# Moving one unit's attention product among the state products, and one state update to an earlier slot, in a fused linear-attention and bilinear FFN kernel

## The chip, the cores and the metric

The kernel runs on one core of one Trainium2 chip. The metric is the device time of one execution in microseconds (us); lower is better. Engines are named as in the profile: PE is TensorE, DVE is VectorE, ACT is ScalarE, POOL is GpSimd, SP is SyncE, which issues nearly all DMAs.

## The reference

Attention over blocks of 64 positions with a decaying state, for 4 batches, 8 heads, 768 positions and head size 64; then a bilinear FFN over the 3072 rows of width 512 with inner width 1536:

```python
for b in range(nb):
    intra = np.einsum('bhic,bhjc->bhij', qb, kb) * Dmask[None]
    intra = np.einsum('bhij,bhjd->bhid', intra, vb)
    inter = np.einsum('bhid,bhde->bhie', qb * lam_pow[None], kv_state)
    out[:, :, sl] = intra + inter
    kv_state = lam_block[None, :, None, None] * kv_state + np.einsum('bhsd,bhse->bhde', kb_dec, vb)
...
return (a * b @ w_out).astype(np.float32)   # a = x @ w_a, b = x @ w_b
```

## The kernel before

The kernel works in blocks of 128 positions, six to a batch: 24 units, numbered 0 to 23. q and k are scaled by powers of lam beforehand, so that the decay drops out of the products: the scores need only a lower-triangular mask, and the state of a unit is the plain sum of k-transposed times v over the units of its batch so far. For each unit there are: the scores kq (line 309, or 561 for the first four units) in two PSUM banks, one for the even and one for the odd heads; the mask m, a DVE product that brings them to SBUF (line 321); the intra product, v times masked scores, eight small column-tiled matmuls (line 346); the inter product, four matmuls with the state of the unit before (line 336); the evacuation of both into xT, the FFN's input (line 353 on ACT, 355 on DVE); and the kv update, four full matmuls (line 360) or eight column-tiled ones (`kv_beside`, line 381), that add to the running sum in one PSUM bank, kvd, followed by `kv_copy`, which takes that sum to SBUF as the unit's state (line 390 on ACT in two halves, line 392 on DVE).

The FFN goes over groups of units (4, 1, 2, 4, 4, 4, 4, 1). For each of 12 slices f of the inner width it makes a (line 428, evacuated by ACT at line 435) and b (line 428, multiplied with a by DVE into ab at line 440), then the output product op (line 449, evacuated by ACT at line 444 and stored). While the FFN of one group runs, the attention work of later units is put between its matmuls by hand: `PLAN` gives for each group pairs of a slot (f, or 12 and on for the halves of the output product) and a piece of work. "P" scales and converts a unit's q, k and v, "T" transposes q and k, "S" makes scores and masks, "V" is the kv update with its copy, "O", "O2" and "Q" are the inter and intra products and evacuations of one or two units, "Q" with the scores and masks of the next two. Each engine executes its instructions in the order in which the program issues them.

PSUM has eight banks: seven are handed out in turn, or at a number given by hand (`at=`), and the eighth holds kvd. A tile that gets a bank waits until the former tile there has been read.

The start phase (lines 505 to 623) does units 0 to 3 before any FFN work, with idle matmuls (`warm`, line 193) on PE between its steps. Lines 599 to 611, the place of the change: the second half of the scores; then the kv products of units 0, 1 and 2, each as a sum of its own over the units up to it (in bank 3, bank 1 and kvd), first the lower two head pairs for all three, then the upper two, with the copies (ACT, ACT, DVE); then the intra products, the inter products and the four evacuations. The fourth mask reads bank 1. The first FFN product needs all four evacuations. In group 2 (units 5 and 6 in the FFN), slot 7 has the kv update of unit 7, slot 12 the "Q" of units 7, 8, 9 and 10, slot 13 the kv update of unit 9 and slot 14 the "O2" of units 9 and 10; the update of unit 8 is made inside `pieces_O` after the intra products:

```python
        if len(us) == 2 and us[0] >= n0 + 3:
            kv_beside(us[1])
        for u, kq in zip(nxt, kqs):
            masks(u, kq)
        if len(us) == 2 and us[0] >= n0 + 3 and us[1] % NB < NB - 1:
            kv_copy(us[1], kv["ps"])
```

Here n0 is 4 and NB is 6.

Of the kernel before, what the change touches and what calls it, by code (L numbers as in the profile page):

```python
# [22 lines left out]
def _bc(ap, dims):  # L23
# [20 lines left out]
    1: [(0, "V", 4), (2, "T", 5), (3, "PK", 6), (6, "PV", 6), (6, "S", 5), (7, "T", 6),  # L44
        (10, "S", 6), (12, "O2", (5, 6)), (13, "P", 7)],
    2: [(0, "V", 6), (1, "T", 7), (1, "P", 8), (4, "T", 8), (5, "P", 9), (6, "S", 7),
        (6, "S", 8), (7, "V", 7), (8, "P", 10), (10, "T", 9), (11, "T", 10),
        (12, "Q", (7, 8, 9, 10)), (12, "P", 11), (13, "V", 9), (14, "P", 12),
        (14, "O2", (9, 10))],
    3: [(3, "S", 11), (3, "S", 12)],  # L50
# [12 lines left out]
def kernel(  # L63
# [12 lines left out]
    B, H, S, D = q.shape  # L76
    BLK = 128
    NB = S // BLK
# [27 lines left out]
    def ps_bank(name, shape, dt, hold=False, ffn=False, at=None):  # L106
        i = bank["next"] if at is None else at
        while i in bank["held"] or (ffn and i == bank["ffn"]):
            i = (i + 1) % 7
        if ffn:  # L110
            bank["ffn"] = i
        bank["next"] = (i + 1) % 7
        if hold:
            bank["held"].add(i)
        return ps_pool.tile(shape, dt, name=name, tag=f"ps{i}")
# [52 lines left out]
    n0 = GROUPS[0]  # L168
# [24 lines left out]
    def warm(n, cols=128):  # L193
        for _ in range(n):
            nc.tensor.matmul(idle_ps[:, :cols], lhsT=idle_sb[:, :128], rhs=idle_sb[:, :cols],  # L195
                             start=True, stop=True, skip_group_check=True)
# [103 lines left out]
    def score_banks():  # L300
        return [ps_bank(f"kq{i}", [128, HP, 128], F32) for i in range(2)]

    def scores(u, kq=None):
        d = U[u]
        kq = kq or score_banks()
        for hp in range(HP):
            for i in range(2):
                p = slice(64 * i, 64 * i + 64)
                nc.tensor.matmul(kq[i][:, hp, :], lhsT=d["kT"][p, hp, :], rhs=d["qT"][p, hp, :],  # L309
                                 start=True, stop=True, skip_group_check=True)  # L310
        return kq

    def masks(u, kq):
        ms = mask(kq)
        U[u]["m"] = lambda i, hp: ms[i][:, hp, :]
# [9 lines left out]
    def o_bank(u):  # L325
        first = "o" not in U[u]
        if first:
            U[u]["o"] = ps_bank("o_ps", [128, HP, 128], F32)
        return first

    def inter(u):
        d = U[u]
        if u % NB > 0:
            first = o_bank(u)
            for hp in range(HP):
                nc.tensor.matmul(d["o"][:, hp, :], lhsT=st_bufs[(u - 1) % 4][:, hp, :, :],  # L336
                                 rhs=d["qT"][:, hp, :], start=(first and hp == 0), stop=True,
                                 skip_group_check=True)

    def intra(u, first=False):  # L340
        d = U[u]
        first = o_bank(u) or first
        for hp in range(HP):
            for i in range(2):
                p = slice(64 * i, 64 * i + 64)
                nc.tensor.matmul(d["o"][p, hp, :], lhsT=d["vb"][:, 2 * hp + i, :],  # L346
                                 rhs=d["m"](i, hp), start=(first and hp == 0),
                                 stop=True, skip_group_check=True)

    def evac_o(u, xT, col, eng="act"):  # L350
        o_ps = U[u].pop("o")
        if eng == "act":
            nc.scalar.copy(xT[:, :, col:col + BLK], o_ps)  # L353
        else:
            nc.vector.tensor_copy(xT[:, :, col:col + BLK], o_ps)

    def kv_mms(ps, w, hps, first):
        d = U[w]
        for hp in hps:
            nc.tensor.matmul(ps[:, hp, :, :], lhsT=d["kn"][:, 2 * hp:2 * hp + 2, :],  # L360
                             rhs=d["vb"][:, 2 * hp:2 * hp + 2, :], start=(first and hp == 0),
                             stop=True, skip_group_check=True)
# [12 lines left out]
    def kv_beside(u):  # L375
        if u % NB == 0 or u % NB == NB - 1:
            kv_update(u)
        for hp in range(HP if 0 < u % NB < NB - 1 else 0):
            for i in range(2):
                p = slice(64 * i, 64 * i + 64)  # L380
                nc.tensor.matmul(kv["ps"][p, hp, i, :], lhsT=U[u]["kn"][:, 2 * hp + i, :],
                                 rhs=U[u]["vb"][:, 2 * hp + i, :],
                                 start=False, stop=True, skip_group_check=True)

    def kv_copy(u, ps, eng="dve"):
        st = st_bufs[u % 4]
        if eng == "act":
            for i in range(2):
                p = slice(64 * i, 64 * i + 64)
                nc.scalar.copy(st[p, :, i, :], ps[p, :, i, :])  # L390
        else:
            nc.vector.tensor_mul(st[:].rearrange("p hp i d -> p hp (i d)"),  # L392
                                 ps[:].rearrange("p hp i d -> p hp (i d)"), bdiag_bc)
# [11 lines left out]
    def pieces_O(us, nxt=()):  # L405
        kqs = [score_banks() for u in nxt]
        for u in us:
            inter(u)
        for u, kq in zip(nxt, kqs):
            scores(u, kq)  # L410
        for u in us:
            intra(u)
            xT, col = xTs[u]
            evac_o(u, xT, col)
        if len(us) == 2 and us[0] >= n0 + 3:
            kv_beside(us[1])
        for u, kq in zip(nxt, kqs):
            masks(u, kq)
        if len(us) == 2 and us[0] >= n0 + 3 and us[1] % NB < NB - 1:
            kv_copy(us[1], kv["ps"])  # L420


# [89 lines left out]
    def scale4(w, i, j):  # L512
        hs = slice(4 * i + 2 * j, 4 * i + 2 * j + 2)
        nc.vector.tensor_mul(
            xs4[w].rearrange("p r (h d) -> p h r d", d=D)[:, hs],
            x4[w, i][:, :, 2 * j:2 * j + 2].rearrange("p r h d -> p h r d"),
            (lp_q if w == "q" else lp_k)[:, NB:, hs, :].rearrange("p r h o -> p h r o")
            .to_broadcast([128, 2, PACK, D]))
        if j == 1:
            staged.pop((w + "4", i))  # L520
# [9 lines left out]
    def part_k(i, j, at):  # L530
        tps = packed_bank("k", at)
        transpose4("k", i, j, tps)
        unpack(i, tps, slice(j, j + 1), "k")
# [18 lines left out]
    def scores4(i, ups, ats):  # L552
        kqs = []
        for up, at in zip(ups, ats):
            kq = [ps_bank(f"kq{par}", [128, HP, 128], F32, at=at[par]) for par in range(2)]
            for uu in range(2):
                cols = slice((2 * up + uu) * BLK, (2 * up + uu + 1) * BLK)
                for j in range(2):
                    for par in range(2):
                        p = slice(64 * par, 64 * par + 64)  # L560
                        nc.tensor.matmul(kq[par][:, 2 * uu + j, :],  # L561
                                         lhsT=xT4["k"][p, 2 * i + j, cols],
                                         rhs=xT4["q"][p, 2 * i + j, cols],
                                         start=True, stop=True, skip_group_check=True)
            kqs.append(kq)
        for up, kq in zip(ups, kqs):
            ms4[i, up] = mask(kq)
# [11 lines left out]
    for at, i, j in ((2, 0, 0), (3, 0, 1), (4, 1, 0)):  # L579
        scale4("k", i, j)  # L580
        part_k(i, j, at)
        warm(3)
    scale4("k", 1, 1)
    for u in range(n0):
        make_vb(u, "pool")
# [6 lines left out]
    sts = [ps_bank(f"kv{u}", [128, HP, 2, D], F32, at=at) for u, at in ((0, 3), (1, 1))]  # L592
    sts.append(kv_bank())

    def kv_part(u, hps):
        for w in range(u + 1):
            kv_mms(sts[u], w, hps, w == 0)

    scores4(1, (0, 1), ((5, 2), (6, 0)))
    for hps in ((0, 1), (2, 3)):  # L600
        for u in range(3):
            kv_part(u, hps)
            if hps[0]:
                kv_copy(u, sts[u], ("act", "act", "dve")[u])
    for u, at in enumerate((4, 5, 2, 6)):
        U[u]["o"] = ps_bank("o_ps", [128, HP, 128], F32, at=at)
    intra(0, True)
    evac_o(0, *xTs[0])
    intra(1, True)
    inter(1)  # L610
    evac_o(1, *xTs[1])
# [74 lines left out]
```

## Time and profile before

| | |
|---|---|
| median of 5 runs | 237.2 us (236.74 to 237.73) |
| the profiled execution | 236.73 us |
| its span, first to last instruction | 235.0 us |
| PE busy | 224.5 us (96%) |
| DVE, ACT, POOL busy | 115.5, 92.9, 48.9 us |
| PE clock granted | 1.000 |
| DMA | 38.32 MB, mean 163 GB/s |

The profile is of one execution. The time of the profiled execution is longer than its span by 1.7 us that lie outside the first and last instruction. Matmuls are pipelined: the ends that the profile shows are modelled, and one matmul's duration (0.22 us for 128 columns, 0.38 for 512) is longer than the distance to the next; costs on PE are read from the distances of starts. A few matmul records are missing, so a group of six can show as five. A merged row gives the start of its first instruction and the time to the end of its last; in brackets stands the idle time of the engine before it and what ended it.

### The profile page before, as it was taken

The numbers are of one execution on the slowest core, as the hardware profiler recorded it, in microseconds if no ns is written. First come the engines' busy times: TensorE is split into PE (matmuls) and PEld (weight loads), VectorE is DVE, ScalarE is ACT, GpSimd is POOL, SyncE is SP. The second block draws the span as 40 slices with busy tenths as digits, with TensorE's granted clock in tenths as the row PEclk, the third lists the DMA queues.
The fourth block names the chain that finished last, engine by engine and source line by source line (L and its number), as shares of the span: only waits on it lengthen the run. The fifth ranks groups of instructions, "written<-read, shape, count | busy, mean of one in ns | idle before, by whom it ended". The sixth has DMA issues, their size and how long they took to land.

```text
span 235.0 us, 4570 instructions
## 1 busy us (share of the span) xinstructions
PE 224.5 (96%) x1775; PEld 125.5 (53%) x1798; DVE 115.5 (49%) x205; ACT 92.9 (40%) x174; POOL 48.9 (21%) x63
## 2 busy tenths in 40 slices
PE   7699999999999899999999999999999999999994
PEld 2474444459687554454554454544454544444493
DVE  0896557536459644884154574144574224332050
ACT  3576753066463633242143242242341243431161
POOL 6041000255336464030333330030300000000000
PEclk9999999999999999999999999999999999999999
DMA  4999999999999999999619949515050220000311
GB/s 152 302 289 347 348 366 277 299 215 284 218 231 208 212 212 249 222 171 231 149 47 210 191 72 234 144 56 126 0 47 0 89 81 13 0 0 5 131 48 46
DMA packets 94278, 38.32 MB, mean 163 GB/s; under 512 B 81200, under 2 KB 89776, under 8 KB 94256
## 3 DMA queue, kind: packets, MB, share of 16 engines
q1 hardware_dynamic: 94112, 38.02, 70.1%
q8 instruction: 14, 0.23, 0.5%
q14 instruction: 8, 0.07, 0.1%
q10 hardware_dynamic: 144, 0.00, 0.0%
HBM read 28.32 MB, written 6.29 MB: 147 GB/s over the span
## 4 chain that ended last, share of the span: by engine, by line
PE 89%; DMA 3%; ACT 3%; DVE 2%; issue 1%; SPq 1%; DVEq 0%; ACTq 0%
PE a_ps L428 27%; PE b_ps L428 26%; PE op L449 25%; DMA k<-in_k_dram 3%; PE kq L309 2%; PE o_ps L346 2%; PE o_ps L336 2%; PE kvd L360 1%; PE tps L295 1%; ACT xT L353 1%; ACT o_sb L444 1%; DVE m L321 1%; SPq L207 1%; ACT st L390 1%; PE kq L561 1%
## 5 line engine op out<-in xcount | busy, mean ns | idle before, releaser
L440 DVE TENSOR_TENSOR ab<-a_sb,b_ps 128x512 bf16<-128x512 bf16 (+2 forms) x96 | 52.5, 552 | 81.3 <-PE b_ps L428 57.9
L428 PE MATMUL a_ps<-xT,wa_sb 128*128 128x512 bf16 (+2 forms) x376 | 76.7, 325 | 1.4 <-ACT xT L353 0.6
L428 PE MATMUL b_ps<-xT,wb_sb 128*128 128x512 bf16 (+2 forms) x382 | 76.8, 325 | 0.0
L435 ACT CAST a_sb<-a_ps 128x512 bf16<-128x512 f32 (+2 forms) x96 | 45.6, 481 | 64.2 <-PE a_ps L428 63.5
L449 PE MATMUL op<-wo_sb,ab 128*128 128x512 bf16 (+2 forms) x299 | 64.0, 362 | 1.1 <-issue 0.6
L428 PEld LDWEIGHTS <-wb_sb 128*128 128x128 bf16 x384 | 34.5, 98 | 29.0 <-issue 0.4
L428 PEld LDWEIGHTS <-wa_sb 128*128 128x128 bf16 x384 | 33.8, 98 | 29.6 <-issue 1.1
L449 PEld LDWEIGHTS <-ab 128*128 128x128 bf16 x312 | 28.7, 98 | 29.9
L321 DVE TENSOR_TENSOR m<-kq,lotri 128x512 bf16<-128x512 f32 x48 | 29.8, 681 | 19.2 <-PE kq L309 18.7
L257 POOL TENSOR_TENSOR qk<-kf,lp_k 128x512 bf16<-128x512 f32 x17 | 18.2, 1072 | 77.8 <-issue 31.6
L444 ACT COPY o_sb<-op 128x512 f32<-128x512 f32 (+2 forms) x26 | 14.2, 554 | 37.9 <-PE op L449 37.9
L262 POOL TENSOR_TENSOR qk<-qf,lp_q 128x512 bf16<-128x512 f32 x20 | 21.7, 1087 | 23.2 <-DMA qf<-in_q_dram 23.2
L353 ACT CAST xT<-o_ps 128x512 bf16<-128x512 f32 x23 | 12.5, 590 | 17.5 <-PE o_ps L346 17.4
L392 DVE TENSOR_TENSOR st<-kvd,bdiag 128x512 bf16<-128x512 f32 x18 | 12.3, 682 | 4.9 <-PE kvd L360 3.8
L297 ACT COPY qkT<-tps 128x1024 bf16<-128x1024 bf16 x7 | 7.1, 1012 | 10.4 <-PE tps L295 10.4
L271 DVE CAST vb<-vf 128x512 bf16<-128x512 f32 x17 | 8.4, 492 | 0.0
L271 POOL CAST vb<-vf 128x512 bf16<-128x512 f32 x7 | 4.8, 684 | 15.8 <-DMA vf<-in_v_dram 13.9
L195 PE MATMUL idle<-idle_sb 128*128 128x128 bf16 (+1 forms) x34 | 6.7, 330 | 1.3 <-DVE idle_sb L190 1.3
L346 PE MATMUL o_ps<-m,vb 128*64 128x128 bf16 x192 | 7.9, 222 | 0.0
L336 PEld LDWEIGHTS <-st 128*128 128x128 bf16 x80 | 5.4, 98 | 2.8
L309 PE MATMUL kq<-qkT 64*128 64x128 bf16 x160 | 6.6, 218 | 0.0
L346 PEld LDWEIGHTS <-vb 128*64 128x64 bf16 x192 | 5.8, 109 | 1.4
(54 smaller groups left out, 83.8 us busy)
## 6 DMA issues: line engine op xcount, KB each, us to landing
vf<-in_v_dram SPq DMA_DIRECT2D x24, 256.0 KB, 5.1
out_dram<-o_sb SPq DMA_DIRECT2D x23, 256.0 KB, 2.0
qf<-in_q_dram SPq DMA_DIRECT2D x20, 256.0 KB, 4.5
kf<-in_k_dram SPq DMA_DIRECT2D x20, 256.0 KB, 5.1
wst<-in_moe_w_a_dram SPq DMA_DIRECT2D x6, 512.0 KB, 8.9
wst<-in_moe_w_b_dram SPq DMA_DIRECT2D x6, 512.0 KB, 8.9
wst<-in_moe_w_out_dram SPq DMA_DIRECT2D x6, 512.0 KB, 8.7
q<-in_q_dram SPq DMA_DIRECT2D x2, 512.0 KB, 5.4
```

The source lines that it names most:

```text
L257: eng_of(eng).tensor_mul(qk[:, 1], raw.pop((u, "k")), lp_k[:, u % NB].to_broadcast([128, H, D]))
L262: eng_of(eng).tensor_mul(U[u]["qk"][:, 0], raw.pop((u, "q")), lp_q[:, u % NB].to_broadcast([128, H, D]))
L271: eng_of(eng).tensor_copy(vb, vf)
L321: nc.vector.tensor_mul(m, kq[i], lotri_bc)
L346: nc.tensor.matmul(d["o"][p, hp, :], lhsT=d["vb"][:, 2 * hp + i, :], rhs=d["m"](i, hp), start=(first and hp == 0), stop=True, skip_group_c ...
L353: nc.scalar.copy(xT[:, :, col:col + BLK], o_ps)
L392: nc.vector.tensor_mul(st[:].rearrange("p hp i d -> p hp (i d)"), ps[:].rearrange("p hp i d -> p hp (i d)"), bdiag_bc)
L428: nc.tensor.matmul(ps[:, :gt], lhsT=w_sb[:, s, f * 128:(f + 1) * 128], rhs=xT[:, s, :gt], start=(s == 0), stop=(s == KS - 1))
L435: nc.scalar.copy(a_sb[:, :gt], ps[:, :gt])
L440: nc.vector.tensor_mul(ab[:, f, :gt], a_sb[:, :gt], ps[:, :gt])
L444: nc.scalar.copy(o_sb[:, lo:hi], op[:, lo:hi])
L449: nc.tensor.matmul(op[:, lo:hi], lhsT=ab[:, f, t * 128:(t + 1) * 128], rhs=wo_sb[:, f, lo:hi], start=(f == 0), stop=(f == FC - 1))
```

## The change

Three edits. In the start phase the idle matmuls after the third part of the k transposes are left out (three matmuls). The intra product of unit 0 and its evacuation move ahead of unit 2's lower kv products and of all upper ones. And the kv update of unit 8 gets a slot of its own, slot 9 of group 2, in the form of four full matmuls with its copy by DVE; the threshold in `pieces_O` rises, so that it is no longer made in slot 12 (the pairs from 9, 10 on keep their `kv_beside`). The number of matmuls changes by the three idle ones and by four full ones in place of eight column-tiled ones; no DMA is added or removed, and the banks handed out are the same.

```diff
     2: [(0, "V", 6), (1, "T", 7), (1, "P", 8), (4, "T", 8), (5, "P", 9), (6, "S", 7),
-        (6, "S", 8), (7, "V", 7), (8, "P", 10), (10, "T", 9), (11, "T", 10),
+        (6, "S", 8), (7, "V", 7), (8, "P", 10), (9, "V", 8), (10, "T", 9), (11, "T", 10),
         (12, "Q", (7, 8, 9, 10)), (12, "P", 11), (13, "V", 9), (14, "P", 12),
...
-        if len(us) == 2 and us[0] >= n0 + 3:
+        if len(us) == 2 and us[0] >= n0 + 5:
             kv_beside(us[1])
         for u, kq in zip(nxt, kqs):
             masks(u, kq)
-        if len(us) == 2 and us[0] >= n0 + 3 and us[1] % NB < NB - 1:
+        if len(us) == 2 and us[0] >= n0 + 5 and us[1] % NB < NB - 1:
             kv_copy(us[1], kv["ps"])
...
         part_k(i, j, at)
-        warm(3)
+        if i == 0:
+            warm(3)
...
     scores4(1, (0, 1), ((5, 2), (6, 0)))
-    for hps in ((0, 1), (2, 3)):
-        for u in range(3):
-            kv_part(u, hps)
-            if hps[0]:
-                kv_copy(u, sts[u], ("act", "act", "dve")[u])
     for u, at in enumerate((4, 5, 2, 6)):
         U[u]["o"] = ps_bank("o_ps", [128, HP, 128], F32, at=at)
+    kv_part(0, (0, 1))
+    kv_part(1, (0, 1))
     intra(0, True)
     evac_o(0, *xTs[0])
+    kv_part(2, (0, 1))
+    for u in range(3):
+        kv_part(u, (2, 3))
+        kv_copy(u, sts[u], ("act", "act", "dve")[u])
     intra(1, True)
     inter(1)
     evac_o(1, *xTs[1])
```

## The prediction, made before the changed kernel was run

> **What bounds the kernel now.** I read the page's chain first, then the timeline of TensorE (PE), ScalarE (ACT) and VectorE (DVE) around the two places that the diff touches, and last the waits of PE.
>
> ```profile
> PE 89%; DMA 3%; ACT 3%; DVE 2%; issue 1%; SPq 1%; DVEq 0%; ACTq 0%
> ```
>
> PE carries the end. From 18.8 us on it has only seven waits, of 0.16 to 0.85 us, in the whole timeline, so a delay or a gain of PE in the start phase, or at one slot later, reaches the end one to one. The start phase, by timeline (start, duration, engine, line, operation; "xN" is a merged group):
>
> ```profile
> 12.13 4.87 DVE L321 TENSOR_TENSOR m<-kq,lotri 128x512 bf16<-128x512 f32 x8 [0.46 <-PE kq L561]
> 14.38 0.67 PE L360 MATMUL kv<-vb,scratch 128*128 128x128 bf16 x6
> 14.89 0.50 PE L360 MATMUL kvd<-vb,scratch 128*128 128x128 bf16 x6
> 15.22 0.50 PE L360 MATMUL kv<-vb,scratch 128*128 128x128 bf16 x6
> 15.56 0.50 PE L360 MATMUL kvd<-vb,scratch 128*128 128x128 bf16 x6
> 15.60 1.51 ACT L390 CAST st<-kv 64x256 bf16<-64x256 f32 x4 [0.98 <-PE kv L360]
> 15.98 0.64 PE L346 MATMUL o_ps<-m,vb 128*64 128x128 bf16 x16
> 16.55 0.40 PE L336 MATMUL o_ps<-scratch,st 128*128 128x128 bf16 x4
> 16.88 0.67 PE L346 MATMUL o_ps<-m,vb 128*64 128x128 bf16 x16
> 17.13 1.60 ACT L353 CAST xT<-o_ps 128x512 bf16<-128x512 f32 x3
> 17.49 0.62 PE L336 MATMUL o_ps<-scratch,st 128*128 128x128 bf16 x8
> 18.78 0.38 PE L428 MATMUL a_ps<-xT,wa_sb 128*128 128x512 bf16 x1 [0.45 <-ACT xT L353]
> ```
>
> The reader should see a chain: DVE makes eight masks without a pause, one each 0.60 us (0.68 us long); ACT then works without a pause from 15.60 to 18.73, four state copies and three evacuations; the first FFN product starts 0.05 us after the last evacuation. The second place, group 2 (units 5 and 6 in the FFN, units 7 to 10 in preparation):
>
> ```profile
> 72.03 2.47 DVE L321 TENSOR_TENSOR m<-kq,lotri 128x512 bf16<-128x512 f32 x4
> 73.95 0.60 PE L428 MATMUL b_ps<-xT,wb_sb 128*128 128x256 bf16 x4
> 74.55 0.60 PE L428 MATMUL a_ps<-xT,wa_sb 128*128 128x256 bf16 x4
> 74.75 0.67 DVE L392 TENSOR_TENSOR st<-kvd,bdiag 128x512 bf16<-128x512 f32 x1
> 77.19 1.46 PE L449 MATMUL op<-wo_sb,ab 128*128 128x512 bf16 x5
> 79.46 2.48 DVE L321 TENSOR_TENSOR m<-kq,lotri 128x512 bf16<-128x512 f32 x4 [1.65 <-PE kq L309]
> 80.05 0.29 PE L381 MATMUL kvd<-vb,qk 128*64 128x64 bf16 x8
> 81.86 0.68 DVE L392 TENSOR_TENSOR st<-kvd,bdiag 128x512 bf16<-128x512 f32 x1
> 82.59 0.38 PE L360 MATMUL kvd<-vb,qk 128*128 128x128 bf16 x4 [0.85 <-DVE st L392]
> 82.81 1.46 PE L449 MATMUL op<-wo_sb,ab 128*128 128x512 bf16 x6
> ```
>
> Here the kv product of unit 9 (82.59) stands still until DVE has copied the state of unit 8 out of the one kv bank, and that copy queues behind four masks: the largest wait of PE after the start.
>
> **What the Trainium skill says.** "PSUM — Partial Sum Buffer", section "Engine vs sequencer instructions": ScalarE and VectorE queues are strict FIFO, and matmuls start in program order. The trace agrees: 82.59 above. So a product put ahead of its mask holds everything behind it. "TensorEngine Tiling (Array Packing)", "Key Properties": a change of the tiling mode drains TensorE. The trace agrees: the last kvd product starts at 15.56 + 0.50 - 0.22 = 15.84, the column-tiled intra product only at 15.98, 0.14 later where the pitch of such products is 0.056 us; and 16.40 to 16.55 on the way back. "TensorE: Matmul & The Clock Gate", Part 1: the clock is at half rate until the array was busy for a window of about 3.4 us, and falls back after an idle one. The trace shows the first half (idle-matmul weight loads at 1.66, 2.08, 2.51, 2.94: 0.43 us apart for 512 columns; eight FFN products later take 1.73 us, 0.216 each); it shows no fall back.
>
> **Change 1: three idle matmuls less.** They take 3 x 0.056 = 0.17 us, at 11.37 just ahead of the scores that start at 11.63. The scores' other needs are done: the k copy on ACT ends at 10.04 + 1.19 = 11.23. So scores, masks (DVE free since 11.67) and all that follows them come about 0.18 us sooner: -0.18. The v casts on POOL are tied to DMAs and don't move, but are in time (units 0 and 1 by 13.44).
>
> **Change 2: unit 0's intra product and evacuation ahead.** Nothing is added but one pair of mode changes (0.1 us each); eight matmuls and one ACT copy move. In the new order the intra product stands behind kv_part(1), which waits for the fourth mask (bank 1): 13.94 + 0.68 = 14.62, shifted 14.44, PE 14.49. Its first four matmuls (0.03 us each) find their masks. The rest needs the fifth and sixth mask; the sixth starts at 15.13, ends at 15.81, shifted 15.63. PE waits until 15.68, and behind it wait unit 2's lower products, all upper kv products, so ACT's copies, so the inter products. Forward, with the old run's latencies:
> - last intra matmul 15.74; ACT evacuates unit 0 from 16.00 (0.26 later, as 17.66 to 17.92 for unit 2) to 16.53 (pitch 1.60 / 3).
> - kvd restarts at 15.89 (0.15 later), six at 0.056; unit 0's two upper products at 16.23 and 16.28; ACT's first copy 0.32 later (15.28 to 15.60 before): 16.60. At 0.38 each, state 0 is whole at 17.35, state 1 at 18.11; unit 1 is evacuated to 18.64.
> - inter(1) waits for state 0: 17.40, last start 17.57. Intra 2 and 3 at 17.73 (0.16 later), inter(2) 18.34 (0.61 later, 16.88 to 17.49 before), inter(3) last start 18.73. ACT evacuates unit 3 at 18.99 to 19.58; the FFN starts at 19.63.
> 19.63 - 18.78 = +0.85 us, change 1 included (alone +1.03). DVE's part (state 2, evacuation of unit 2 at 18.77 to 19.46) is just covered, and the cast of the second weight on DVE is then done by 20.15 where its product needs it at 21.36. Weights are fetched as before: no DMA is issued by a moved step, and those of group 0 find PE later, so earlier by comparison. Bounds: +0.5 if the latencies shrink or the upper products are served sooner, +1.1 if the 0.18 is not gained.
>
> **Change 3: kv update of unit 8 in slot 9.** Removed at slot 12: eight column-tiled products, about 0.11 us by their starts (80.05 to 80.16), and DVE's copy of state 8 behind the four masks. So unit 9's product, which could start when the six op products are done (80.27 + 6 x 0.216 = 81.57), no longer waits until 82.59: -1.02. Added after b of f = 9: four full products, 0.22 us. But they write the kv bank, which DVE has to have copied for unit 7, and that copy stands behind the four masks of units 7 and 8 and one ab product: 74.75 + 0.67 = 75.42. PE would be there at 74.55 (where it was held by the last mask already), and starts at 75.47: 0.92 of waiting. In the build's instruction list this first product waits on DVE. So +0.92 + 0.22 = +1.14 against -1.13: zero. The next thing late would be unit 9's state for the inter products: masks then end at 83.08, a v cast at 83.42, state 9 at 84.03; PE arrives at unit 10's inter at 84.34. Covered. Bounds: -0.9 if the wait isn't there, +0.3 if the state copies come later still. Unit 8's k buffer comes free some 4 us sooner, so POOL's scaling of unit 12 (held for 3.48 us until 80.48) and later loads on SP's queue start sooner; PE waits for none of them here: nothing.
>
> **Sum:** +0.85 + 0.0 = +0.85 us. Profiled execution: 236.73 + 0.85 = 237.6. The median of the runs, 237.2, lies 0.47 above it, so 238.05, forecast 238.1.
>
> **Rivals.**
> - A: unit 8 gains, the front loses. If slot 9 waits less (the state copy of unit 7 comes sooner, or PE arrives later than I place it), -0.9 to -0.3 sets off the front: 237.15 to 237.75. For it: unit 9's wait is real and goes; against: the mask queue at 72.03 to 74.50 is as real. Chance 0.12.
> - B, the faster side: the new places come after DVE's masks, not ahead of them. Then the intra product fills ACT's idle 0.98 us: unit 0's upper products at 15.49, ACT's copies from 15.87, FFN at 18.90 (+0.12), and unit 8 gains -1.13 + 0.22 = -0.91: 237.2 - 0.8 = 236.4. It decides where the sixth mask ends before 14.9 and state 7 before 74.55; the trace has 15.63 and 75.42. Chance 0.07.
> - C: with fewer idle matmuls and longer gaps the clock falls to half for one 3.4 us window, which loses 1.7 us (an estimate from that page's window): 237.2 + 0.85 + 1.7 = 239.8. Against: between 6.59 and 9.9 PE held full pitch with 24 x 0.056 = 1.3 us of matmuls in 3.3; the new stretch 8.6 to 12.0 has 2.0. Chance 0.05.
>
> **How the numbers follow.** My forecast has 0.76. A measurement of this kernel can tell about 0.3% (0.71 us) from no change. Of the 0.76, with its own range +0.45 to +1.3 us, I put 0.60 above 0.71 and 0.16 below. Slower: 0.60 + 0.05 = 0.65. Same: 0.16 + 0.12 = 0.28. Faster: 0.07. The range 237.1 to 238.9 takes in nearly all of A and the bounds of the sizes, and leaves out B, C and tails.
>
> **What would show it.** Right: the scores at 11.45; a PE gap of over half a us inside unit 0's intra product, ended by DVE's mask; the first L353 on ACT at about 16.0 ahead of the four L390, which start at 16.6; the first FFN product near 19.6; a PE wait of about 0.9 us on DVE's state copy in slot 9, and none before unit 9's product. Wrong: an FFN start by 18.8, or slot 9 without a wait.

## The result and the profile after

The changed kernel takes 238.21 us (median of 24 runs, 237.22 to 239.0), the kernel before 236.91 us in the same comparison (43 runs, 236.13 to 238.25). The ratio is 1.0048, 95% interval 1.0036 to 1.0061: slower by 1.14 us (0.85 to 1.45); the two medians lie 1.30 us apart, and the text goes by the ratio, which has the interval. The profiled execution took 238.6 us with a span of 236.9 us. It is 1.87 us longer than the profiled execution of before, more than the typical loss, so its parts have to be weighed against the medians below.

First the page of the changed kernel, with the chain of work that ended last, by engine:

```profile
span 236.9 us, 4556 instructions
PE 84%; DMA 6%; DVE 4%; issue 3%; ACT 2%; SPq 1%; DVEq 0%
```

PE still carries the end, but DMA and DVE have taken five points of the chain from it. Where, the chain in order of time shows. The start phase (start, duration, what):

```profile
12.06 3.69 DVE m L321 x6
15.75 0.04 issue
15.79 0.27 PE o_ps L346 x3
16.06 0.44 PE kvd L360 x6
16.50 0.34 PE kv L360 x6
16.84 0.34 PE kvd L360 x6
17.17 0.34 PE o_ps L346 x8
17.52 0.39 PE o_ps L336 x4
17.91 0.57 PE o_ps L346 x16
18.47 0.57 PE o_ps L336 x8
19.04 0.02 issue
19.07 0.59 ACT xT L353
19.66 0.04 issue
19.70 0.38 PE a_ps L428
```

Six masks run to their end before the last three matmuls of unit 0's intra product may go, and 18 kv products and the other three units' intra and inter products stand behind these three. ACT in the same stretch, from its timeline:

```profile
16.10 0.59 ACT L353 CAST xT<-o_ps 128x512 bf16<-128x512 f32 x1 [1.56 <-PE o_ps L346]
16.71 1.51 ACT L390 CAST st<-kv 64x256 bf16<-64x256 f32 x4
```

It now waits 1.56 us where it waited 0.98, and the state copies start at 16.71 instead of 15.60.

Then PE's waits after the start, from PE's timeline, without four of 0.16 or 0.17 us:

```profile
58.11 0.38 PE L428 MATMUL a_ps<-xT,wa_sb 128*128 128x128 bf16 x4 [0.93 <-DVE ab L440]
76.98 0.38 PE L360 MATMUL kvd<-vb,qk 128*128 128x128 bf16 x4 [0.93 <-DVE st L392]
103.54 0.40 PE L309 MATMUL kq<-qkT 64*128 64x128 bf16 x8 [0.20 <-DMA qkT<-qk]
```

The second is unit 8's product in slot 9, 0.93 us for the 0.92 that was foreseen; unit 9's product, at 84.10, no longer waits. The prediction foresaw neither the first nor the third. The kernel before has none at the place of the third, and at the first place it has this:

```profile
56.53 0.38 PE L428 MATMUL a_ps<-xT,wa_sb 128*128 128x128 bf16 x4 [0.28 <-DVE ab L440]
```

The distance of the two profiled executions, read at the same instruction of each, puts sizes to all of this:

| at | before | after | distance | added since the row above |
|---|---|---|---|---|
| scaling of k on DVE begins | 8.86 | 8.98 | +0.12 | the k load came later |
| first FFN product | 18.78 | 19.70 | +0.92 | +0.80, the start phase |
| inter of unit 5 | 60.97 | 62.55 | +1.58 | +0.66, the wait at 58 |
| inter of units 9 and 10 | 84.11 | 85.62 | +1.51 | -0.07, unit 8's edit |
| kv product of unit 12 | 102.56 | 104.44 | +1.88 | +0.37, the wait at 103.5 |
| inter of unit 23 | 200.38 | 202.26 | +1.88 | 0 |

For the wait at 58 us, DVE and POOL of both kernels. The kernel before:

```profile
55.60 0.68 DVE L257 TENSOR_TENSOR qk<-kf,lp_k 128x512 bf16<-128x512 f32 x1
55.75 1.43 POOL L257 TENSOR_TENSOR qk<-kf,lp_k 128x512 bf16<-128x512 f32 x1 [1.43 <-ACT a_sb L435]
```

The changed kernel:

```profile
56.27 1.04 POOL L257 TENSOR_TENSOR qk<-kf,lp_k 128x512 bf16<-128x512 f32 x1 [1.44 <-ACT a_sb L435]
56.52 1.34 DVE L257 TENSOR_TENSOR qk<-kf,lp_k 128x512 bf16<-128x512 f32 x1
```

Both scale a unit's k, DVE that of unit 6 and POOL that of unit 7. Whichever begins second is held until the first is nearly done: POOL before (1.43 instead of 1.04 us), DVE after (1.34 instead of 0.68). The Trainium skill, "SBUF — State Buffer", section "Who interferes with whom", has just this: a VectorE instruction with two SBUF inputs contends with a GpSimd instruction that reads SBUF, and the order of issue decides who is blocked. DVE's next instructions are the ab products that give PE its banks back, so PE stands still; POOL has time. DVE's scaling comes when the chain of PE and DVE gets there, and the start phase has moved that by 0.92 us. POOL's moved by 0.52 here. The brackets name an ACT copy, but in the profiles of runs 1 and 7 they name the load of k, and over all 14 profiles POOL begins between 55.75 and 56.45 us, whether the start was moved or not. So it goes with the load, as far as the profiles tell.

The ten profiles that can be compared agree on this. In the seven of kernels with the old start order and unit 6 scaled in slot 3 (before, runs 1, 3, 4, 8, 9, 10), DVE is first by 0.15 to 0.69 us and PE waits 0.27 or 0.28 us. In the three with the whole delay in the start (changed, runs 2 and 6), POOL is first by 0.14 to 0.41 us and PE waits 0.78 to 1.04 us.

### The profile page after: what moved, and what is told of

Same layout as the page of the kernel before. It is cut to its first block, busy times and chain, and to the rows that moved or that the text cites. A ratio compares the mean times of both kernels' runs of the same rounds, so it can differ in the third digit from the quotient of the medians.

```text
span 236.9 us, 4556 instructions
## 1 busy us (share of the span) xinstructions
PE 225.4 (95%) x1768; PEld 125.8 (53%) x1791; DVE 116.4 (49%) x205; ACT 92.9 (39%) x174; POOL 48.6 (21%) x63
## 4 chain that ended last, share of the span: by engine, by line
PE 84%; DMA 6%; DVE 4%; issue 3%; ACT 2%; SPq 1%; DVEq 0%
PE op L449 26%; PE a_ps L428 24%; PE b_ps L428 24%; DMA k<-in_k_dram 3%; PE o_ps L346 3%; DMA qkT<-qk 3%; DVE m L321 3%; PE o_ps L336 2%; PE kq L309 2%; PE kvd L360 2%; PE tps L295 1%; ACT o_sb L444 1%; SPq L207 1%; ACT xT L353 0%; DVE ab L440 0%
## 5 line engine op out<-in xcount | busy, mean ns | idle before, releaser
L271 DVE CAST vb<-vf 128x512 bf16<-128x512 f32 x17 | 9.0, 529 | 0.0
L346 PE MATMUL o_ps<-m,vb 128*64 128x128 bf16 x192 | 8.4, 223 | 0.4 <-DVE m L321 0.4
L271 POOL CAST vb<-vf 128x512 bf16<-128x512 f32 x7 | 4.3, 614 | 16.1 <-DMA vf<-in_v_dram 14.0
```

Of the source, the lines that this page charges most:

```text
L271: eng_of(eng).tensor_copy(vb, vf)
```

## The experiments

Each run was compared with the kernel before on the same chip (236.4 to 236.6 us there). A ratio of 1.001 is 0.24 us.

**1. The idle matmuls alone.**

```diff
-        warm(3)
+        if i == 0:
+            warm(3)
```

> Only the three idle matmuls are left out. Theory (the start phase's chain of scores and masks moves forward by the 0.17 us that they take): 0.1 to 0.2 us faster than before, first FFN product 0.15 us sooner against the last k transposes than before. Rival (the clock falls, or the chain is held elsewhere): 0.5 us or more slower, or no change at all.

Measured: 236.35 us, ratio 0.9999 (0.9985 to 1.0013). The start does gain: from the scaling of k (8.96) to the first FFN product (18.70) it takes 9.74 us, against 9.92 before, 0.18 less, as worked out. Whether the end has it can't be told: 0.18 us is 0.08%, and the interval holds both that and nothing. In the profiled execution PE came to unit 14's scores early and waited 1.36 us for a transpose, until 102.47; but that execution, 237.61 us, is the longest of the 14. The theory holds for the start and is open for the whole.

**2. The intra product alone.** The diff is the last hunk of the change.

> Only unit 0's intra product and evacuation are moved ahead. Theory (PE stands still for the sixth mask and holds the kv products behind it): FFN start 1.0 us later, and, since the changed kernel's trace shows a DVE scaling of unit 6's k stretched from 0.68 to 1.34 us by a POOL scaling that began just before it, up to 0.65 us more at about 57 us: 1.0 to 1.7 us slower. Rival (the start costs nothing beyond its own time in the whole program, the 0.65 belongs to unit 8's edit or to chance): exactly the start's delay, 0.85 to 1.05 us.

Measured: 237.80 us, ratio 1.0059 (1.0042 to 1.0077), slower by 1.4 us (1.0 to 1.8). The first FFN product starts at 19.74 with the k scaling at 8.85: 0.97 later than before, close to the 1.03 of the prediction. DVE's scaling of unit 6 took 1.19 us and PE waited 0.78 us at 57.99. The interval just touches the rival's 0.85 to 1.05; run 6 decides.

**3. Unit 8's update alone.** The first two hunks of the change.

> Only unit 8's kv update is moved to slot 9. Theory of the prediction (the wait for the state copy moves from unit 9's product to unit 8's, one for one): within 0.1 us of before. With the knock-on seen in the changed kernel's trace (slot 12 comes 1.1 us later, the first DMA transpose waits for it, and so does the whole DMA queue, up to unit 14's transposed k and q, 0.37 us late at slot 7 of group 3): 0.2 to 0.5 us slower. Rival (unit 9's wait goes and nothing takes its place): 0.9 us faster.

Measured: 236.71 us, ratio 1.0011 (1.0001 to 1.0021), slower by 0.26 us (0.0 to 0.5). No gain of 0.9, so that rival is out; between the two theories, nothing and 0.2 to 0.5 us, the interval doesn't decide. Its profile shows a wait of 0.57 us in slot 9, none at unit 9, and 0.68 us at unit 14's scores.

**4. Unit 8's update one slot later.** With the raised threshold of the change.

```diff
-        (6, "S", 8), (7, "V", 7), (8, "P", 10), (10, "T", 9), (11, "T", 10),
+        (6, "S", 8), (7, "V", 7), (8, "P", 10), (10, "V", 8), (10, "T", 9), (11, "T", 10),
```

> Unit 8's kv update in slot 10 instead of 9, ahead of the transposes of unit 9; the rest as before. Theory (in slot 9 it is early by one a and b product: the copy of unit 7's state ends at 75.42 and slot 10 begins at 75.42): no PE wait at either product, 0.22 us of full products against 1.13 us that go: 0.8 to 0.95 us faster. Rival (the copies of the states queue on DVE in any order, the wait only shifts): within 0.2 us of before.

Measured: 236.50 us, ratio 1.0005 (0.9991 to 1.0019). Both waits are gone from PE, as foreseen, and the time is not. From the inter product of unit 5 to that of units 9 and 10 it takes 21.57 us, in runs 8 and 11 too, against 22.48 in run 10, which has unit 8's update in its old place: 0.91 less. So the theory was right on the place and wrong on the worth. Where the gain goes, the profile shows in the extreme: it is of the longest of the 22 executions, 239.38 us, at a mean clock of 0.991.

```profile
102.64 0.40 PE L309 MATMUL kq<-qkT 64*128 64x128 bf16 x8 [2.25 <-DMA qkT<-qk]
105.46 1.89 PE L428 MATMUL b_ps<-xT,wb_sb 128*128 128x512 bf16 x4
107.16 1.04 PE L428 MATMUL a_ps<-xT,wa_sb 128*128 128x512 bf16 x4
```

PE waits 2.25 us for unit 14's transpose, and soon after that its clock falls: from 103.77 to 107.16 eight products of 512 columns start 0.43 us apart instead of 0.216, which costs another 1.7 us. Neither size is typical; the other 21 executions took 237.02 us or less.

**5. Half of the intra product moved.** The lower two head pairs, whose masks are ready, at the new place; the upper two and the evacuation behind the kv products. The diff is against the changed kernel's order; the idle matmuls and unit 8's update are as before.

```diff
     kv_part(1, (0, 1))
-    intra(0, True)
-    evac_o(0, *xTs[0])
+    intra(0, True, (0, 1))
     kv_part(2, (0, 1))
...
         kv_copy(u, sts[u], ("act", "act", "dve")[u])
+    intra(0, False, (2, 3))
+    evac_o(0, *xTs[0])
```

> As before, but the half of unit 0's intra product whose masks are ready (lower two head pairs) stands where the change puts it, and the half that needs the fifth and sixth mask stays behind the kv products, with the evacuation. Theory (the loss in the start is the wait for the sixth mask with everything behind it): only one more pair of mode changes, 0.1 to 0.3 us slower. Rival (the place itself costs, by mode changes and by the products pushed back): 0.6 to 1.0 us slower.

Measured: 237.17 us, ratio 1.0031 (1.0020 to 1.0041), slower by 0.73 us (0.5 to 1.0): in the rival's range. The start phase itself lost 0.29 us (from 9.04 to 19.25, 10.21 against 9.92), in the theory's. PE around the half product, from its timeline:

```profile
14.54 0.67 PE L360 MATMUL kv<-vb,scratch 128*128 128x128 bf16 x6
15.14 0.30 PE L346 MATMUL o_ps<-m,vb 128*64 128x128 bf16 x4
15.38 0.51 PE L360 MATMUL kvd<-vb,scratch 128*128 128x128 bf16 x6
```

There is no wait in it. The last kv product starts at 14.99 and the first kvd product at 15.38, 0.39 later where products in a row are 0.056 apart: 0.33 more, of which the four matmuls of 0.03 us are 0.12 and the two changes of the tiling mode 0.21. So of the 0.97 us that the whole move costs in the start (run 2), about 0.3 is the place and the rest the wait for the masks. Why the whole lost 0.4 more than the start is not settled: in the profiled run (236.69 us) DVE was first at 56.07 and POOL began 0.02 us later, so that a slightly earlier load would turn it round; but that was not counted over the runs.

**6. A pause and nothing else.** Four matmuls that read the finished xT, ahead of the first FFN product of the kernel before.

```diff
     natural_k((3,), (0, 1, 2, 3), 3)
+    pause = ps_bank("pause", [128, 512], F32, at=1)
+    for _ in range(4):
+        nc.tensor.matmul(pause, lhsT=idle_sb[:, :128], rhs=gx[0][:, 3, :],
+                         start=True, stop=True, skip_group_check=True)
+    bank["next"] = 4
```

> The kernel before with four idle 512-column matmuls that read the finished xT, put ahead of the first FFN product: PE is delayed by 4 x 0.216 = 0.86 us there and by nothing else. Theory (a delay of PE by that much puts the DVE scaling of unit 6's k behind a POOL scaling that a DMA releases, and DVE is stretched by 0.65 us): 1.1 to 1.6 us slower, with the DVE scaling at 1.3 us and a PE wait of 0.9 us near 57 us in the profile. Rival (a start delay reaches the end one to one): 0.8 to 0.95 us slower, DVE scaling 0.68 us.

Measured: 237.97 us, ratio 1.0063 (1.0049 to 1.0076), slower by 1.49 us (1.16 to 1.80), for 0.86 us of pause. POOL and DVE of this run:

```profile
56.45 1.04 POOL L257 TENSOR_TENSOR qk<-kf,lp_k 128x512 bf16<-128x512 f32 x1 [1.54 <-ACT a_sb L435]
56.59 1.46 DVE L257 TENSOR_TENSOR qk<-kf,lp_k 128x512 bf16<-128x512 f32 x1
```

POOL is first by 0.14 us, DVE is held for 0.78, PE waits at 58.30. A plain delay in the start therefore costs 0.6 us (0.3 to 0.9) more than itself, without any of the three edits.

**7. The changed kernel with unit 6 scaled sooner.**

```diff
-    1: [(0, "V", 4), (2, "T", 5), (3, "PK", 6), (6, "PV", 6), (6, "S", 5), (7, "T", 6),
+    1: [(0, "V", 4), (1, "PK", 6), (2, "T", 5), (6, "PV", 6), (6, "S", 5), (7, "T", 6),
```

> The changed kernel with the scaling of unit 6's k and q (slot 3 of group 1) issued in slot 1, so that DVE comes to it about 0.9 us sooner, ahead of POOL's scaling. Theory: the stretched DVE instruction and the PE wait at 58 us go, 0.3 to 0.7 us faster than the changed kernel, that is 0.5 to 0.9 us slower than the kernel before. Rival (the wait at 58 us was chance of one profile, or DVE and POOL collide elsewhere): as the changed kernel, 1.1 to 1.3 us slower than before.

Measured: 236.87 us, ratio 1.0022 (1.0013 to 1.0030), slower than before by 0.52 us; the changed kernel is slower by 1.14, so 0.62 of it went. DVE and POOL:

```profile
54.49 0.68 DVE L257 TENSOR_TENSOR qk<-kf,lp_k 128x512 bf16<-128x512 f32 x1
55.78 1.04 POOL L257 TENSOR_TENSOR qk<-kf,lp_k 128x512 bf16<-128x512 f32 x1 [1.44 <-DMA kf<-in_k_dram]
```

They no longer meet, and the PE wait is gone, the 0.28 us that the kernel before has there too. With run 6 and the profiles counted above this settles the wait at 58 us: it belongs to the shift, and it is no chance of one profile. Not all of the 0.62 us does, though: the edit alone on the kernel before was not run, and run 11 gains about 0.5 us by it against run 9, whose start is not delayed.

**8. The two parts that gain on PE, together.** The kernel before with the edits of runs 1 and 4.

> The kernel before without the three idle matmuls and with unit 8's kv update in slot 10; the start order as before. Theory (the two gains add): 0.9 to 1.1 us faster than before. Rival (one of them is given back later): 0.3 us or less.

Measured: 236.57 us, ratio 0.9998 (0.9987 to 1.0009). Nothing is left. PE in its timeline around unit 14:

```profile
99.46 0.39 PE L336 MATMUL o_ps<-qkT,st 128*128 128x128 bf16 x4
99.78 0.40 PE L309 MATMUL kq<-qkT 64*128 64x128 bf16 x8
101.08 0.40 PE L309 MATMUL kq<-qkT 64*128 64x128 bf16 x8 [0.90 <-DMA qkT<-qk]
```

In the kernel before:

```profile
101.12 0.39 PE L336 MATMUL o_ps<-qkT,st 128*128 128x128 bf16 x4
101.44 0.62 PE L309 MATMUL kq<-qkT 64*128 64x128 bf16 x16
```

PE came to this place 1.66 us sooner than before: 1.1 us by the two edits, and about 0.6 because the profile of before has a slow cast near 70 us (see the last section). The second eight scores, those of unit 14, wait for its transposed q and k. SP's queue shows why these did not come sooner too. This kernel:

```profile
92.17 0.58 SPq L126 DMA_DIRECT2D qf<-in_q_dram  x1
92.79 0.92 SPq L126 DMA_DIRECT2D kf<-in_k_dram  x1
93.81 0.73 SPq L126 DMA_DIRECT2D vf<-in_v_dram  x1
94.66 2.41 SPq L281 DMA_TRANSPOSE qkT<-qk  x1
```

The transpose stands behind three loads of unit 16 in a queue that is busy back to back since about 69 us, and lands 6.4 us after its issue (at 101.04, by the chain). In the kernel before it is issued at 94.74, though its PE is 1.6 us later; in runs 1, 3 and 4, whose PE was early too, at 95.5 to 96.2. In these profiles the queue did not come sooner when PE did.

**9. The same with unit 14's transpose ahead of those loads.**

```diff
+PLAN[3] = [e for e in PLAN[3] if e not in ((1, "P", 13), (3, "P", 14))]
+PLAN[3] += [(1, "PK", 13), (1, "PK", 14), (1, "PV", 13), (3, "PV", 14)]
```

> The combined kernel (no third group of idle matmuls, unit 8's update in slot 10, start order as before) with one thing more: in group 3 the scaling and the DMA transpose of unit 14 are issued in slot 1 right after those of unit 13, ahead of the loads of unit 16 on SP's queue. Theory (the 1.1 to 1.6 us that PE had gained by slot 7 of group 3 were given back there, to the transpose of unit 14, which sits behind three loads on a queue that is busy back to back): the transpose is issued near 92 and lands before 99.5, no PE wait, 0.8 to 1.3 us faster than before. Rival (the queue and the DMA engines as a whole set the pace, so the wait comes back at this or the next transposes): within 0.4 us of before.

Measured: 235.30 us, ratio 0.9944 (0.9925 to 0.9962), faster by 1.3 us (0.9 to 1.8). SP's queue of this kernel (its line numbers are two higher), then PE:

```profile
91.35 3.03 SPq L283 DMA_TRANSPOSE qkT<-qk  x2
94.43 0.57 SPq L128 DMA_DIRECT2D qf<-in_q_dram  x1
```

```profile
100.02 0.39 PE L338 MATMUL o_ps<-qkT,st 128*128 128x128 bf16 x4
100.34 0.62 PE L311 MATMUL kq<-qkT 64*128 64x128 bf16 x16
```

Sixteen score matmuls in one row and no wait. The gain of run 8's edits was real and was given back at this one place; the rival is out.

**10. The earlier transpose alone,** on the kernel before.

> The kernel before with the earlier transpose of unit 14 alone. Theory (in the kernel before PE comes to unit 14's scores at about the time its transpose lands, and waits only in some runs): 0 to 0.4 us faster. Rival (the order of the queue is worth the gain by itself): 0.8 us or more faster.

Measured: 236.18 us, ratio 0.9984 (0.9976 to 0.9992), faster by 0.4 us, so the rival is out. Run 9's gain is therefore not the queue's order by itself: 0.9 of 1.3 us are the two edits, now let through. The likely reason for its own 0.4, not shown, is that the kernel before waits for this transpose in part of its executions, though not in the profiled one.

**11. Run 9 and unit 6 scaled sooner.**

> As the combined kernel with the earlier transpose, and unit 6's scaling issued in slot 1 of group 1, so that DVE does it before POOL's scaling begins. Theory: the PE wait of 0.28 us at 56.5 goes too, 0.2 to 0.4 us faster than without this edit, 1.1 to 1.6 us faster than before. Rival (given back to a transpose): no faster than without it.

Measured: 234.69 us, ratio 0.9924 (0.9906 to 0.9941), faster by 1.8 us (1.4 to 2.2). This version beats both kernels. Against run 9 it is 0.5 us better, by ratios whose intervals overlap.

**12. The changed kernel with both edits.**

> The changed kernel with both of these edits (unit 14's transpose ahead of three loads, unit 6's scaling in slot 1). Theory: of the changed kernel's loss only the start's 0.82 us is left, less the 0.28 us wait at 56.5 that before has: 0.3 to 0.6 us slower than before. Rival (slot 9's wait costs beyond the wait itself, by the whole DMA queue): 0.8 us or more slower.

Measured: 236.72 us, ratio 1.0005 (0.9996 to 1.0014), slower than before by 0.1 us. That is less than the theory had, but it doesn't mean that the change has become almost free: the two edits also speed up kernels without it (0.4 us in run 10, about 0.5 from run 9 to run 11), which the theory left out.

The fair partner is run 11. It has both edits too, and differs from run 12 by the moved intra product and by slot 10 instead of 9. Read on PE, the first costs 0.99 us (first FFN product 10.72 us after the scaling of k, against 9.73). The second costs 0.73 (from the inter product of unit 5 to that of units 9 and 10, 22.30 us with slot 9 in run 3, 21.57 with slot 10), 1.7 together. By the ratios run 12 is 1.9 us slower, with intervals of 0.4 us either way for run 11 and 0.2 for run 12. With the meeting of DVE and POOL and the late transpose out of the way, what PE loses reaches the end about one to one.

## Why the prediction was right, and where it was short

The forecast was 238.05 us, +0.85; measured are 238.21 us and +1.14 (0.85 to 1.45). The direction and the mechanism of the main term were right. That the time itself is met within 0.2 us is in part luck: the forecast started from 237.2, a median of five runs, 0.29 us above the 236.91 of the 43, and its loss is 0.29 us too small.

- **Idle matmuls, -0.18.** Right in the start phase (0.18 in run 1). What it is worth at the end is below what run 1 can tell. The clock stayed at 1.000 in both profiled executions; rival C did not occur. But the fall of the clock that it feared does exist in this program: the prediction saw none in the trace, and run 4's profile has one, after a wait of 2.25 us.
- **Intra product ahead, +1.03.** Right: 0.97 in run 2, and with the idle matmuls gone 0.80 for the 0.85 that was summed. The mechanism is as described: PE stood still until the sixth mask (15.79, forecast 15.68), the evacuation began at 16.10 (16.00), the copies at 16.71 (16.60), the FFN at 19.70 (19.63), 0.1 of each being the later k of this run. Run 5 divides the 0.97: about 0.3 of place and mode changes, the rest the wait.
- **A delay in the start reaches the end "one to one".** This is the step that failed, and the loss is larger than the sum by it, as far as the interval tells, which just reaches 0.85; run 6 shows the step by itself. It holds for PE's own queue (run 12 against run 11). It doesn't hold where two engines hold each other up and one of them is driven by DMA: 0.86 us became 1.49 in run 6. The trace of before shows POOL's stretched 1.43 us, which the prediction does not mention; it should have asked what happens if the order turns, which 0.15 us decided there.
- **Unit 8 in slot 9, zero.** Right on PE, term by term: a wait of 0.93 us for the 0.92, none left at unit 9, and -0.07 in all; without the slow cast, which both these profiles have, it is -0.18 (22.30 in run 3 against 22.48 in run 10), and the wait in slot 9 is 0.57 us. The queues were costed at nothing: "PE waits for none of them here". In the profile of the changed kernel they are not nothing. SP's first transpose, which waits for slot 12, was issued at 81.68 instead of 79.03, unit 14's at 97.31 instead of 94.74, and PE waited for it (+0.37). But over many executions this is not shown to be a cost of the change: the earlier transpose gains 0.4 us on the kernel before (run 10) and 0.4 on the changed kernel (run 12 against run 7). Run 3 has 0.26 us (0.0 to 0.5) for the edit alone.
- **PE "has only seven waits, of 0.16 to 0.85 us, in the whole timeline".** The list of waits leaves one out. From 72.16 to 74.55 in the trace of before, four a and b products start 0.60 us apart instead of 0.44, held by DVE, and PE loses 0.65 us in pieces too short to be listed. The prediction saw that PE was held there, but not that the slow cast of this one execution was behind it (last section).
- **Rivals A and B.** Neither occurred. B's second half, the gain of unit 8's update without a wait, was made in run 4 by one slot more, and even then no gain came out: its price of -0.91 was right on PE and overlooked that PE then meets the transpose. So the faster side was less likely than it seemed.

The measured parts add only roughly: runs 1, 2 and 3 sum to about +1.6 us where the whole change has +1.14. Their intervals are wide enough for that, so no cause is sought in it.

## What to carry to other kernels

Before a product is moved forward in an in-order queue, take the end of its last input and list what stands behind it: here three matmuls of 0.03 us held 18 kv products and four state copies. A shift on the critical engine can be worth more than itself where it turns the order of two engines that hold each other up (run 6), and a gain less than itself where the next thing needed comes from a queue that did not speed up with it (run 8); look for both within the length of the shift. Before two variants are compared, give both the edits that lift their waits: run 12 looks almost free beside the kernel before, and is 1.9 us slower than run 11. And when a wait is removed and the time stays, look for the next wait by name in the trace, and lift that one, before the edit is called useless: runs 8 and 9 differ by the place of one unit's scaling and transpose and by 1.3 us.

## What the runs showed of the hardware that was not expected

- Two elementwise products with both inputs in SBUF, one on DVE and one on POOL, exclude each other for nearly the whole instruction: 0.68 us became 1.34 and 1.46 on DVE when POOL was first by 0.25 and 0.14 us, and 1.04 became 1.43 on POOL when DVE was first by 0.15. In both of the first two DVE ends about 0.55 us after POOL.
- Casts from SBUF to SBUF on DVE do the same. The v cast at 70 to 72 us takes 0.42 to 0.44 us in seven of the 14 profiles and up to 1.27 in the others; in that of before a POOL scaling had begun 0.05 us ahead of it, in that of run 10, the same kernel up to there, the cast was first:

```profile
70.45 1.04 POOL L257 TENSOR_TENSOR qk<-kf,lp_k 128x512 bf16<-128x512 f32 x1 [2.39 <-DMA kf<-in_k_dram]
70.50 1.27 DVE L271 CAST vb<-vf 128x512 bf16<-128x512 f32 x1
```

```profile
70.58 0.42 DVE L273 CAST vb<-vf 128x512 bf16<-128x512 f32 x1
70.97 1.04 POOL L259 TENSOR_TENSOR qk<-kf,lp_k 128x512 bf16<-128x512 f32 x1 [2.51 <-PE kq L311]
```

From the inter product of unit 5 to that of units 9 and 10 these two kernels take 23.14 and 22.48 us. So single profiles differ by over half a us in this stretch, and parts of this size need the medians. The changed kernel's profile has the slow cast too (1.19 us), so the table above is not bent by it.

- A pair of changes between full and column-tiled products costs about 0.2 us (in run 5, 0.39 us from the last full product to the next, less 0.056 for the usual distance and 0.12 for the four matmuls between).
- Once, in run 4, a wait of 2.25 us was followed, about 1.1 us after its end, by 3.4 us in which PE ran at half its clock (granted 0.51 from 103.7 to 107.2). Run 1's wait of 1.36 us was not followed by such a stretch.
- A DMA transpose of one unit took 6.4 us from issue to landing in run 8, behind loads that kept the queue full.
